# Three split float32r matmuls per product, or one on plain float32: the gate, value and output products of an attention and gated-MLP kernel

## The chip, the cores and the metric

The kernel runs on one core of a Trainium2 chip. The metric is the time of one execution in device microseconds (us); three runs of the kernel before gave 731.21 to 731.88 us with a median of 731.56. The core has five engines that run side by side and meet at semaphores: TensorE (PE in the profile, its weight loads PEld), VectorE (DVE), ScalarE (ACT), GpSimd (POOL) and SyncE (SP), the last of which issues most transfers here.

## The reference

Two stages follow one another. The first is chunked attention with 4 batches, 8 heads, 768 positions and 64 dimensions a head: each chunk of 32 queries sees 8 memory tokens and a window of 56 keys. The second is a gated MLP on the 3072 resulting tokens of 512 features, with an RMS norm ahead of it and a hidden width of 1536. Results are float32.

```
x = attn_out.transpose(0, 2, 1, 3).reshape(B * S, H * D)
rms = np.sqrt(np.mean(x * x, axis=-1, keepdims=True) + 1e-06)
xn = x / rms * rms_g
g = xn @ w_gate
silu = g * (1.0 / (1.0 + np.exp(-g)))
val = xn @ w_val
return (silu * val @ w_out).astype(np.float32)
```

The products called gate, value and output below are `xn @ w_gate`, `xn @ w_val` and the last one. The three weight matrices lie in memory as float64, two 32-bit words to a value, which the kernel turns into float32 itself; all else is float32.

## The kernel before, in words

**Tiling.** The 3072 tokens are cut into 8 blocks (NBLK) of 384 tokens (HT), a block being half a batch. The hidden width is cut into 12 slices f of 128 (NF), the 512 features into 4 slices kt of 128 (NKT). For a block and an f, `moe_in` (L556 to L564) makes the gate product pg and the value product pv, each a 128 x 384 tile of PSUM summed over the 4 kt; the weights are stationary, the block's features xs are moving. `moe_out` (L596 to L600) adds f's share of the output product to three tiles po of 128 tokens x 512 features, one for each 128 tokens of the block; there the hidden values are stationary and the rows of w_out are moving.

**The split.** TensorE is given float32r operands (F32R). Each operand is held as a high part (the value rounded to float32r) and a low part (the rest). `PASS = ((0, 0), (0, 1), (1, 0))` (L554) makes three matmuls of every product: high x high, high x low, low x high. The parts are made as follows.

- Block features: `stage_xt` transposes them on TensorE (xT, L440), `stage_xh` scales them by rms_g into xh (ScalarE or VectorE), `stage_xl` makes xl on VectorE (L450).
- Weights, in 24 chunks: `w_load` (token Z) brings words into a staging tile ws; `w_open`, `w_clamp`, `w_sign` and `w_shift` (J, F, f, I) turn two words into one float32 in a second tile wy; `w_high` (H) casts it into the high part wh on ScalarE, `w_low` (L) subtracts on VectorE and leaves the low part wl (L532).
- Hidden values: `silu_a` (tanh on ScalarE, L568), `silu_b` and `moe_m` (VectorE, L572 and L575) make t; `moe_hh` casts it into hh on ScalarE (L227), `moe_hl` subtracts on VectorE into hl (L584). hh and hl have one buffer each.

With two parts for each weight the weights take twice their size, so those of f 5 to 9 and of f 10 and 11 get their room only when the pools early and stage are closed in the middle of the run (`late_weights`, LATE).

**Order.** The first two blocks run under a written order: the string ORDER (L47 to L64) is a list of tokens, each a step of one engine with its number, and every engine takes its steps in that order. It interleaves the attention of the first eight units with the decoding of the weights and with the first products. W8, W5, W4, W9 and W6 are so many small matmuls on zeros (`warm`, L307). After it, loops over blocks and f issue the work (L857 to L900): gate, value, then the output product of the f before, with the attention of the block after next spread over the gaps; TensorE's order is pinned to the program's, and a planner places the rest. At the end of a block `split_x` makes the next block's features; the last f of the last block goes through `finish`, which works in pieces of 128 tokens.

**Attention on plain float32.** Scores (L318) and attention times values (L368) are plain float32 matmuls already, with 64 stationary columns and 64 or 65 moving ones, and the transposes (L237, L240, L348, L440) are float32 too.

Of the kernel before, what the change touches and what calls it, by code (L numbers as in the profile page):

```python
# [9 lines left out]
F32R = mybir.dt.float32r  # L10
# [13 lines left out]
P = 128  # L24
# [35 lines left out]
l9 I h10 i10 o9 Ha I Z j10 Ha L g11 k10a l10 J L o10 h11 F i11 Z J f v11 L f I F g12 Ha j11 I k11a  # L60
Z J l11 v12 f Ha F L h12 i12 o11 L j12 Z J I g13 f k12a F Ha I v13 L Ha l12 L h13 Z J o12 i13 f
j13 F g14 k13a I l13 Ha L Z J o13 f h14 F I v14 i14 Ha L g15 j14 Z J k14a f l14 F v15 h15 I i15 Ha
g16 j15 J L f F o14 I Ha L v16 k15a l15 h16 o15 i16 j16
# [4 lines left out]
def tile_kernel(ctx: ExitStack, tc: tile.TileContext, q, k, v, mem_k, mem_v,  # L68
# [11 lines left out]
    dram = ctx.enter_context(tc.tile_pool(name="dram", bufs=1, space=bass.MemoryType.DRAM))  # L80
# [5 lines left out]

    def new_weights(pool, a, z):
        for k, (f, n) in enumerate(WGROUPS):
            if a <= f < z:
                for w in "gvo":  # L90
                    for part in range(2):
                        wt[part, w, k] = pool.tile([P, n * DM], F32R, name=f"w{'hl'[part]}_{w}{k}")
    new_weights(const, 0, LATE[0][0])
# [337 lines left out]
    def stage_x(tiles, xh, xl, kt):  # L431

        t = stage_xt(tiles, kt)
        stage_xh(t, xh, kt)
        stage_xl(t, xh, xl, kt)
# [7 lines left out]
    def stage_xh(t, xh, kt, e="a"):  # L443
        if e == "a":
            nc.scalar.activation(xh[:, kt], t[:, 0:HT], AF.Copy, scale=rg[:, kt:kt + 1])
        else:
            nc.vector.tensor_scalar(out=xh[:, kt], in0=t[:, 0:HT], scalar1=rg[:, kt:kt + 1], scalar2=None, op0=ALU.mult)

    def stage_xl(t, xh, xl, kt):
        nc.vector.scalar_tensor_tensor(out=xl[:, kt], in0=t[:, 0:HT], scalar=rg[:, kt:kt + 1], in1=xh[:, kt].bitcast(F32),  # L450
                                       op0=ALU.mult, op1=ALU.subtract)

# [6 lines left out]
    wfirst = [next(c for c, (w, k) in enumerate(wchunks) if WGROUPS[k][0] == late[0]) for late in LATE]  # L459
# [4 lines left out]
    def weight(part, w, f, kt=0):  # L464

        k, i, n = fgroup[f]
        t = wt[part, w, k]
        return t[:, i * DM:(i + 1) * DM] if w == "o" else t[:, (kt * n + i) * P:(kt * n + i + 1) * P]

    def w_load():  # L470
# [6 lines left out]
        d = wst[c] = {}  # L477
        j = c - wfirst[1]
        if j < 0:
            pool = stage if c % 3 else p1  # L480
            tag = str(c % 3) if c % 3 else ""
            s = pool.tile([P, 2, DM, 2], U32, name=f"ws{c}", tag="ws" + tag)
            s = s.rearrange("p n f t -> p (n f) t")[:, 0:n * DM]
        elif j % 3 == 2:
            s = p1.tile([P, DM, 2], U32, name=f"ws{c}", tag="wy")
        else:
            if j % 3 == 0:
                wst["pair"] = p1.tile([P, 2, DM, 2], U32, name=f"ws{c}", tag="ws")
            s = wst["pair"][:, j % 3]
        d.update(n=n, low=s[:, :, 0], high=s[:, :, 1])  # L490
        if w == "o":
            nc.sync.dma_start(out=s.rearrange("p (i f) t -> p i (f t)", i=n),
                              in_=w_out[f * P:(f + n) * P].bitcast(U32).rearrange("(i p) f -> p i f", p=P))
        else:
            src = w_gate if w == "g" else w_val
            nc.sync.dma_start(out=s.rearrange("p (a f) t -> p a (f t)", a=NKT),
                              in_=src.bitcast(U32)[:, 2 * f * P:2 * (f + n) * P].rearrange("(a p) f -> p a f", p=P))

    def w_open(c):

        d = wst[c]
        if c >= wfirst[1]:
            y = obuf(f"wy{c}")
        else:
            pool = stage if c % 3 else p1
            tag = str(c % 3) if c % 3 else ""
            y = pool.tile([P, 2 * DM], F32, name=f"wy{c}", tag="wy" + tag)[:, 0:d["n"] * DM]
# [13 lines left out]
    def w_shift(c):  # L521
        d = wst[c]
# [4 lines left out]
    def w_high(c, e="a"):  # L527
        copy(e, wt[(0,) + wchunks[c]], wst[c]["y"])

    def w_low(c):  # L530
        w = wchunks[c]
        nc.vector.tensor_tensor(out=wt[(1,) + w], in0=wst.pop(c)["y"], in1=wt[(0,) + w].bitcast(F32), op=ALU.subtract)  # L532
        if c + 1 == wfirst[1]:
            stage_cm.__exit__(None, None, None)
            late_weights(1, "left")

    def w_next(fn, *e):

        c = wpos[fn]
        wpos[fn] += 1  # L540
        fn(c, *e)

    wpos.update({fn: 0 for fn in (w_open, w_clamp, w_sign, w_shift, w_high, w_low)})

    def late_weights(i, side):
        late = ctx.enter_context(tc.tile_pool(name=f"late{i}", bufs=1, side=side, reuse_waits="tile"))
        new_weights(late, *LATE[i])

# [5 lines left out]
    PASS = ((0, 0), (0, 1), (1, 0))  # L554

    def moe_in(n, f, xs, last=False):  # L556
        ps = psum_a(f"p{n}") if last else psum_m(n, f"p{n}")
        cnt = 0
        for kt in range(NKT):
            for a, c in PASS:  # L560
                on_pe(nc.tensor.matmul(ps[:, 0:HT], lhsT=weight(a, n, f, kt), rhs=xs[c][:, kt],  # L561
                                 start=cnt == 0, stop=cnt == 3 * NKT - 1))
                cnt += 1
# [10 lines left out]
    def moe_m(t, vv):  # L574
        nc.vector.tensor_tensor(out=t, in0=t, in1=vv, op=ALU.mult)  # L575

    def moe_hh(t, e="a"):
        hh = p1.tile([P, HT], F32R, name="hh", tag="hh")
        copy(e, hh, t)
        return hh  # L580

    def moe_hl(t, hh):
        hl = p1.tile([P, HT], F32R, name="hl", tag="hl")
        nc.vector.tensor_tensor(out=hl, in0=t, in1=hh.bitcast(F32), op=ALU.subtract)  # L584
# [11 lines left out]
    def moe_out(f, h, po):  # L596
        for i in range(NT):
            for n, (a, c) in enumerate(PASS):
                on_pe(nc.tensor.matmul(po[i], lhsT=h[a][:, i * P:(i + 1) * P], rhs=weight(c, "o", f),  # L599
                                 start=f == 0 and n == 0, stop=f == NF - 1 and n == 2))  # L600
# [11 lines left out]
    def finish(f, g, vv, po, blk):  # L612
# [3 lines left out]
        hh = p1.tile([P, HT], F32R, name="hh", tag="hh")  # L616
        hl = p1.tile([P, HT], F32R, name="hl", tag="hl")
        for i in range(NT):
            c = slice(i * P, (i + 1) * P)
            nc.vector.tensor_tensor(out=t[:, c], in0=t[:, c], in1=vv[:, c], op=ALU.mult)  # L620
            nc.scalar.copy(hh[:, c], t[:, c])
            nc.vector.tensor_tensor(out=hl[:, c], in0=t[:, c], in1=hh[:, c].bitcast(F32), op=ALU.subtract)
        for i in range(NT):
            c = slice(i * P, (i + 1) * P)
            o = obuf(f"ob{i}")
            for n, (a, b) in enumerate(PASS):
                on_pe(nc.tensor.matmul(po[i], lhsT=(hh, hl)[a][:, c], rhs=weight(b, "o", f), start=False, stop=n == 2))
# [94 lines left out]
    xs01 = []  # L722
    for i in range(2):
        xs01.append([p1.tile([P, KW + VW], F32R, name=f"x{'hl'[k]}{i}", tag=t)[:, 0:NKT * HT].rearrange("p (a t) -> p a t", a=NKT)
                     if t == "B" else p1.tile([P, NKT, HT], F32R, name=f"x{'hl'[k]}{i}", tag=t)
                     for k, t in enumerate((("xh", "xl"), ("A", "B"))[i])])
# [202 lines left out]
```

## Time and profile before

| | |
|---|---|
| runs shown (three) | 731.21 to 731.88 us, median 731.56 |
| span of the profiled execution | 729.8 us, first to last instruction |
| that execution's own time | not listed apart from the runs |
| TensorE busy | 715.1 us (98%), 5136 matmul records |
| weight loads | 656.6 us (90%) |
| VectorE, ScalarE, GpSimd busy | 380.0, 287.8 and 36.4 us |
| granted TensorE clock, mean | 0.995 of full |
| chain by line | value 28%, output 28%, gate 27% of the span |

The page gives busy time per engine, the span in 40 slices, the chain of work that ended last (followed back from the last instruction), and groups of instructions: line, engine, operation, output and inputs, count, then busy time, mean ns of one, and idle time before it with its releaser. A shape "128*64 128x96" is rows and columns of the stationary operand, then the moving one. In a timeline a row is start, length, engine, line, operation, names, count; in rows by stretch of time it is the stretch, its length, busy time of PE, PEld, DVE, ACT and POOL with counts in brackets, the granted clock, the share of the DMA engines and GB/s. Rows of waits are: who waited, for what, us in total, times, longest.

### The profile page before, as it was taken

The numbers are of one execution on the slowest core, as the hardware profiler recorded it, in microseconds if no ns is written. First come the engines' busy times: TensorE is split into PE (matmuls) and PEld (weight loads), VectorE is DVE, ScalarE is ACT, GpSimd is POOL, SyncE is SP. The second block draws the span as 40 slices with busy tenths as digits, with TensorE's granted clock in tenths as the row PEclk, the third lists the DMA queues.
The fourth block names the chain that finished last, engine by engine and source line by source line (L and its number), as shares of the span: only waits on it lengthen the run. The fifth ranks groups of instructions, "written<-read, shape, count | busy, mean of one in ns | idle before, by whom it ended". The sixth has DMA issues, their size and how long they took to land.

```text
span 729.8 us, 13052 instructions
## 1 busy us (share of the span) xinstructions
PE 715.1 (98%) x5136; PEld 656.6 (90%) x5136; DVE 380.0 (52%) x725; ACT 287.8 (39%) x600; POOL 36.4 (5%) x143
## 2 busy tenths in 40 slices
PE   8889999999999999999999999999999999999997
PEld 7778999999989999899999999989998999999996
DVE  4888999865645443444535353445434543332222
ACT  4899676643452323422333232432234222341112
POOL 3300000001000000000000000000000000000000
PEclk8999999999999999999999999999999999999999
DMA  8994563414412320122212123021311210010001
GB/s 173 203 259 141 173 202 116 132 37 102 85 37 68 55 50 22 62 46 42 43 38 66 23 45 61 20 66 31 66 29 34 64 32 20 20 44 0 1 1 43
DMA packets 143173, 50.20 MB, mean 69 GB/s; under 512 B 126984, under 2 KB 134536, under 8 KB 143112
## 3 DMA queue, kind: packets, MB, share of 16 engines
q1 hardware_dynamic: 139832, 44.49, 26.6%
q10 hardware_dynamic: 3280, 4.88, 1.8%
q8 instruction: 40, 0.66, 0.4%
q14 instruction: 21, 0.17, 0.1%
HBM read 43.06 MB, written 6.29 MB: 68 GB/s over the span
## 4 chain that ended last, share of the span: by engine, by line
PE 92%; ACT 3%; DMA 3%; DVE 1%; issue 0%; POOL 0%; ACTq 0%; SPq 0%; POOLq 0%
PE pv L561 28%; PE po L599 28%; PE pg L561 27%; PE s L318 3%; PE o L368 3%; PE xT L440 1%; PE pT L348 1%; DMA ws<-in_moe_w_val_dram 1%; DMA memV<-in_mem_v_dram 1%; DMA vw<-in_v_dram 1%; ACT junk L398 0%; ACT ws L508 0%; ACT pt L227 0%; DMA kv<-in_v_dram 0%; ACT qb L227 0%
## 5 line engine op out<-in xcount | busy, mean ns | idle before, releaser
L561 PE MATMUL pv<-xh,wh_v 128*128 128x384 f32 x384 | 132.8, 346 | 0.0
L561 PE MATMUL pg<-xh,wh_g 128*128 128x384 f32 x384 | 129.7, 338 | 0.7 <-DVE t L572 0.7
L561 PE MATMUL pv<-xh,wl_v 128*128 128x384 f32 x384 | 129.5, 337 | 0.6 <-DVE wl_v L532 0.6
L561 PE MATMUL pg<-xh,wl_g 128*128 128x384 f32 x384 | 129.5, 337 | 0.0
L561 PE MATMUL pg<-xl,wh_g 128*128 128x384 f32 x384 | 129.3, 337 | 0.0
L561 PE MATMUL pv<-xl,wh_v 128*128 128x384 f32 x384 | 129.3, 337 | 0.0
L572 DVE SCALAR_TENSOR_TENSOR t<-t,pg 128x384 f32<-128x384 f32 x96 | 53.1, 553 | 138.6 <-ACT t L568 138.5
L227 ACT CAST hh<-t 128x384 fp32r<-128x384 f32 x95 | 48.7, 512 | 174.9 <-PE po L599 165.3
L599 PE MATMUL po<-wh_o,hh 128*128 128x512 f32 x285 | 113.8, 399 | 0.3
L599 PE MATMUL po<-wh_o,hl 128*128 128x512 f32 x285 | 113.1, 397 | 0.0
L599 PE MATMUL po<-wl_o,hh 128*128 128x512 f32 x285 | 112.1, 393 | 0.0
L584 DVE TENSOR_TENSOR hl<-t,hh 128x384 fp32r<-128x384 f32 x95 | 52.9, 557 | 100.7 <-ACT hh L227 95.7
L568 ACT ACTIVATE t<-pg 128x384 f32<-128x384 f32 x96 | 47.2, 492 | 135.9 <-PE pg L561 130.8
L575 DVE TENSOR_TENSOR t<-t,pv 128x384 f32<-128x384 f32 x95 | 52.5, 552 | 64.9 <-PE pv L561 64.4
L561 PEld LDWEIGHTS pg<-xh,wh_g 128*128 128x128 f32 x384 | 72.1, 188 | 4.4 <-DVE t L572 0.9
L561 PEld LDWEIGHTS pg<-xl,wh_g 128*128 128x128 f32 x384 | 72.1, 188 | 3.6
L561 PEld LDWEIGHTS pv<-xh,wh_v 128*128 128x128 f32 x384 | 72.1, 188 | 2.4
L561 PEld LDWEIGHTS pv<-xh,wl_v 128*128 128x128 f32 x384 | 72.2, 188 | 0.9 <-DVE wl_v L532 0.9
L561 PEld LDWEIGHTS pv<-xl,wh_v 128*128 128x128 f32 x384 | 72.2, 188 | 0.3
L561 PEld LDWEIGHTS pg<-xh,wl_g 128*128 128x128 f32 x384 | 72.1, 188 | 0.0
L599 PEld LDWEIGHTS po<-wh_o,hl 128*128 128x128 f32 x285 | 53.5, 188 | 14.1 <-DVE hl L584 1.8
L599 PEld LDWEIGHTS po<-wh_o,hh 128*128 128x128 f32 x285 | 53.5, 188 | 10.0 <-ACT hh L227 1.7
(112 smaller groups left out, 772.9 us busy)
## 6 DMA issues: line engine op xcount, KB each, us to landing
kn<-in_k_dram SPq DMA_DIRECT2D x96, 52.0 KB
qn<-in_q_dram SPq DMA_DIRECT2D x96, 48.0 KB
out_dram<-ob ACTq DMA_DIRECT2D x18, 256.0 KB
ws<-in_moe_w_gate_dram SPq DMA_DIRECT2D x4, 1024.0 KB
ws<-in_moe_w_val_dram SPq DMA_DIRECT2D x4, 1024.0 KB
ws<-in_moe_w_out_dram SPq DMA_DIRECT2D x4, 1024.0 KB
kv<-in_v_dram SPq DMA_DIRECT2D x48, 84.0 KB
kv<-in_v_dram SPq DMA_DIRECT2D x48, 70.0 KB
```

Source lines behind the costliest of these rows:

```text
L227: return nc.scalar.copy(out, in_)
L318: on_pe(nc.tensor.matmul(s[64 * par:64 * par + 64, o:o + KC], lhsT=qb[:, c].rearrange("p s q -> p (s q)"), rhs=kw[:, c], start=True, stop= ...
L348: on_pe(nc.tensor.transpose(out=t[:, i * P:(i + 1) * P], in_=pe[:, i * P:(i + 1) * P], identity=ident))
L368: on_pe(nc.tensor.matmul(o[64 * par:64 * par + 64, c0:c0 + D + 1], lhsT=pt[:, i, 2 * par + hh].rearrange("p c q -> p (c q)"), rhs=d["v"][: ...
L440: on_pe(nc.tensor.transpose(out=t[:, i * P:(i + 1) * P], in_=tiles[i][:, kt * P:(kt + 1) * P], identity=ident))
L561: on_pe(nc.tensor.matmul(ps[:, 0:HT], lhsT=weight(a, n, f, kt), rhs=xs[c][:, kt], start=cnt == 0, stop=cnt == 3 * NKT - 1))
L568: nc.scalar.activation(t, g, AF.Tanh, scale=0.5)
L572: nc.vector.scalar_tensor_tensor(out=t, in0=t, scalar=1.0, in1=g, op0=ALU.add, op1=ALU.mult)
L575: nc.vector.tensor_tensor(out=t, in0=t, in1=vv, op=ALU.mult)
L584: nc.vector.tensor_tensor(out=hl, in0=t, in1=hh.bitcast(F32), op=ALU.subtract)
L599: on_pe(nc.tensor.matmul(po[i], lhsT=h[a][:, i * P:(i + 1) * P], rhs=weight(c, "o", f), start=f == 0 and n == 0, stop=f == NF - 1 and n == 2))
```

## The change

Every product is one matmul on float32 operands, where it was three on float32r. The high and low parts are gone: features are one tile xs (two buffers, by turns), hidden values one tile h (two buffers), weights one tile each. The decoded weights are written straight into their final tile, whose room is there from the start; the late pools and their bookkeeping are gone. In ORDER the tokens H, L, D, k and l are struck out; the others keep their sequence.

```
-    PASS = ((0, 0), (0, 1), (1, 0))
+    def product(out, lhsT, rhs, start, stop):
+        on_pe(nc.tensor.matmul(out, lhsT=lhsT, rhs=rhs, start=start, stop=stop))
...
         for kt in range(NKT):
-            for a, c in PASS:
-                on_pe(nc.tensor.matmul(ps[:, 0:HT], lhsT=weight(a, n, f, kt), rhs=xs[c][:, kt],
-                                 start=cnt == 0, stop=cnt == 3 * NKT - 1))
-                cnt += 1
+            product(ps[:, 0:HT], weight(n, f, kt), xs[:, kt], kt == 0, kt == NKT - 1)
...
         for i in range(NT):
-            for n, (a, c) in enumerate(PASS):
-                on_pe(nc.tensor.matmul(po[i], lhsT=h[a][:, i * P:(i + 1) * P], rhs=weight(c, "o", f),
-                                 start=f == 0 and n == 0, stop=f == NF - 1 and n == 2))
+            product(po[i], h[:, i * P:(i + 1) * P], weight("o", f), f == 0, f == NF - 1)
...
     def moe_m(t, vv):
-        nc.vector.tensor_tensor(out=t, in0=t, in1=vv, op=ALU.mult)
-
-    def moe_hh(t, e="a"):
-        hh = p1.tile([P, HT], F32R, name="hh", tag="hh")
-        copy(e, hh, t)
-        return hh
-
-    def moe_hl(t, hh):
-        hl = p1.tile([P, HT], F32R, name="hl", tag="hl")
-        nc.vector.tensor_tensor(out=hl, in0=t, in1=hh.bitcast(F32), op=ALU.subtract)
-        return hh, hl
+        h = p2.tile([P, HT], F32, name="h", tag="h")
+        nc.vector.tensor_tensor(out=h, in0=t, in1=vv, op=ALU.mult)
+        return h
...
-    def stage_xl(t, xh, xl, kt):
-        nc.vector.scalar_tensor_tensor(out=xl[:, kt], in0=t[:, 0:HT], scalar=rg[:, kt:kt + 1], in1=xh[:, kt].bitcast(F32),
-                                       op0=ALU.mult, op1=ALU.subtract)
...
-            y = pool.tile([P, 2 * DM], F32, name=f"wy{c}", tag="wy" + tag)[:, 0:d["n"] * DM]
+        y = wt[wchunks[c]]
...
-    def w_high(c, e="a"):
-        copy(e, wt[(0,) + wchunks[c]], wst[c]["y"])
-
-    def w_low(c):
-        w = wchunks[c]
-        nc.vector.tensor_tensor(out=wt[(1,) + w], in0=wst.pop(c)["y"], in1=wt[(0,) + w].bitcast(F32), op=ALU.subtract)
-        if c + 1 == wfirst[1]:
-            stage_cm.__exit__(None, None, None)
-            late_weights(1, "left")
...
     def finish(f, g, vv, po, blk):
...
-        hh = p1.tile([P, HT], F32R, name="hh", tag="hh")
-        hl = p1.tile([P, HT], F32R, name="hl", tag="hl")
+        h = p2.tile([P, HT], F32, name="h", tag="h")
         for i in range(NT):
             c = slice(i * P, (i + 1) * P)
-            nc.vector.tensor_tensor(out=t[:, c], in0=t[:, c], in1=vv[:, c], op=ALU.mult)
-            nc.scalar.copy(hh[:, c], t[:, c])
-            nc.vector.tensor_tensor(out=hl[:, c], in0=t[:, c], in1=hh[:, c].bitcast(F32), op=ALU.subtract)
+            nc.vector.tensor_tensor(out=h[:, c], in0=t[:, c], in1=vv[:, c], op=ALU.mult)
```

More of the change, by code (lines that the diff above doesn't have):

```diff
@@ new lines @@
+Q2a S1 E0 n2d K2d c2a Z J P0 M1 p5 w2 t3 C0a f m0a S2 a1 Q3a T3 p6 M2 E1 U4 a2 P1 w3 O0 n3d m1a F C1a K3d V4g
+c3a O1 E2 X0 I U5 S3 x0 V5g J X1 u0 U6 P2 x1 M3 p7 W8 C2a Z f m2a w5 a3 O2 u1 E3 V6g P3 X2 t4 F m3a U7 x2 C3a
+I T4 Q4a w6 u2 O3 K4d c4a N0 n4d V7g X3 S4 x3 w4 u3 t5 M4 a4 T5 Q5a T6 c5a n5d Y0 K5d Z K6d t6 w7 n6d c6a y0
+E4 S5 Q6a P4 M5 r0 S6 z0 C4a m4a W4 a5 J M6 t7 E5 f T7 a6 Q7a F P5 n7d K7d m5a A0 c7a I C5a S7 B0a A1 M7 W5
+B1a E6 a7 Z A2 J A3 O4 B2a f W9 X4 E7 B3a x4 P6 F W6 C6a m6a u4 O5 Z J I O6 X5 f P7 g0 X6 x5 x6 u5 C7a m7a u6
@@ new lines @@
+v0 h0 F N1 Z I O7 J X7 i0 x7 g1 j0 u7 Y1 v1 y1 f Z h1 r1 z1 o0 J i1 F j1 A12 A11 I B12a A13 B11a g2 Z B13a A10
+v2 B10a h2 J i2 o1 f j2 g3 J F f v3 I h3 i3 Z o2 f j3 F g4 I v4 h4 i4 J Z F g5 f j4 I o3 v5 F Z J h5 o4 i5 I
+g6 j5 f v6 J Z h6 f o5 i6 F j6 g7 F I J o6 f Z h7 v7 F i7 I g8 j7 I v8 Z h8 i8 J o7 j8 g9 F Z J o8 f h9 f v9 F
+i9 I g10 J j9 Z f F v10 I h10 i10 o9 I Z j10 g11 J o10 h11 F i11 Z J f v11 f I F g12 j11 I Z J v12 f F h12 i12
+o11 j12 Z J I g13 f F I v13 h13 Z J o12 i13 f j13 F g14 I Z J o13 f h14 F I v14 i14 g15 j14 Z J f F v15 h15 I
@@ L64 @@
+i15 g16 j15 J f F o14 I v16 h16 o15 i16 j16
 """
@@ L85, in tile_kernel @@
     wt = {}
[L87 to L93, printed above, removed]
+    for i, (_, n) in enumerate(WGROUPS):
+        for w in "gvo":
+            wt[w, i] = const.tile([P, n * DM], F32, name=f"w_{w}{i}")
     ident = const.tile([P, P], F32, name="ident")
@@ L429, in stage_n, with stage_x @@
         stage_nz(x, sr, "a")
[L431 to L435, printed above, removed]
+    def stage_x(tiles, xs, kt):
+        stage_xh(stage_xt(tiles, kt), xs, kt)
     def stage_xt(tiles, kt):
@@ L441, in stage_xt, with stage_xh @@
         return t
-    def stage_xh(t, xh, kt, e="a"):
+    def stage_xh(t, xs, kt, e="a"):
         if e == "a":
-            nc.scalar.activation(xh[:, kt], t[:, 0:HT], AF.Copy, scale=rg[:, kt:kt + 1])
+            nc.scalar.activation(xs[:, kt], t[:, 0:HT], AF.Copy, scale=rg[:, kt:kt + 1])
         else:
-            nc.vector.tensor_scalar(out=xh[:, kt], in0=t[:, 0:HT], scalar1=rg[:, kt:kt + 1], scalar2=None, op0=ALU.mult)
-    def stage_xl(t, xh, xl, kt):
-        nc.vector.scalar_tensor_tensor(out=xl[:, kt], in0=t[:, 0:HT], scalar=rg[:, kt:kt + 1], in1=xh[:, kt].bitcast(F32),
-                                       op0=ALU.mult, op1=ALU.subtract)
+            nc.vector.tensor_scalar(out=xs[:, kt], in0=t[:, 0:HT], scalar1=rg[:, kt:kt + 1], scalar2=None, op0=ALU.mult)
     LOW = 0.936 * 2.0 ** -29
     wchunks = [(w, k) for k in range(len(WGROUPS)) for w in "gvo"]
-    wfirst = [next(c for c, (w, k) in enumerate(wchunks) if WGROUPS[k][0] == late[0]) for late in LATE]
     fgroup = {f + i: (k, i, n) for k, (f, n) in enumerate(WGROUPS) for i in range(n)}
@@ L462, in tile_kernel, with weight, staged @@
     wpos = {"load": 0}
-    def weight(part, w, f, kt=0):
+    def weight(w, f, kt=0):
         k, i, n = fgroup[f]
-        t = wt[part, w, k]
+        t = wt[w, k]
         return t[:, i * DM:(i + 1) * DM] if w == "o" else t[:, (kt * n + i) * P:(kt * n + i + 1) * P]
+    def staged(c, what, shape, dtype):
+        pool = stage if c % 3 else p1
+        return pool.tile(shape, dtype, name=f"{what}{c}", tag=f"{what}{c % 3}")
     def w_load():
@@ L476, in w_load @@
         f, n = WGROUPS[k]
[L477 to L490, printed above, removed]
+        s = staged(c, "ws", [P, 2, DM, 2], U32).rearrange("p n f t -> p (n f) t")[:, 0:n * DM]
+        wst[c] = dict(n=n, low=s[:, :, 0], high=s[:, :, 1])
         if w == "o":
@@ L525, in w_shift, with w_next @@
                                        op0=ALU.logical_shift_left, op1=ALU.bitwise_or)
-    def w_high(c, e="a"):
-        copy(e, wt[(0,) + wchunks[c]], wst[c]["y"])
-    def w_low(c):
-        w = wchunks[c]
-        nc.vector.tensor_tensor(out=wt[(1,) + w], in0=wst.pop(c)["y"], in1=wt[(0,) + w].bitcast(F32), op=ALU.subtract)
-        if c + 1 == wfirst[1]:
-            stage_cm.__exit__(None, None, None)
-            late_weights(1, "left")
-    def w_next(fn, *e):
+    def w_next(fn):
         c = wpos[fn]
         wpos[fn] += 1
[L541 to L547, printed above, removed]
+        fn(c)
+    wpos.update({fn: 0 for fn in (w_open, w_clamp, w_sign, w_shift)})
     segments = [(0, FC)] + [(blk, 0) for blk in range(2, NBLK)]
-    PASS = ((0, 0), (0, 1), (1, 0))
+    def product(out, lhsT, rhs, start, stop):
+        on_pe(nc.tensor.matmul(out, lhsT=lhsT, rhs=rhs, start=start, stop=stop))
     def moe_in(n, f, xs, last=False):
         ps = psum_a(f"p{n}") if last else psum_m(n, f"p{n}")
-        cnt = 0
         for kt in range(NKT):
-            for a, c in PASS:
-                on_pe(nc.tensor.matmul(ps[:, 0:HT], lhsT=weight(a, n, f, kt), rhs=xs[c][:, kt],
-                                 start=cnt == 0, stop=cnt == 3 * NKT - 1))
-                cnt += 1
+            product(ps[:, 0:HT], weight(n, f, kt), xs[:, kt], kt == 0, kt == NKT - 1)
         return ps[:, 0:HT]
@@ L625, in finish @@
             o = obuf(f"ob{i}")
-            for n, (a, b) in enumerate(PASS):
-                on_pe(nc.tensor.matmul(po[i], lhsT=(hh, hl)[a][:, c], rhs=weight(b, "o", f), start=False, stop=n == 2))
+            product(po[i], h[:, c], weight("o", f), False, True)
             rows = slice(blk * HT + i * P, blk * HT + (i + 1) * P)
@@ L721, in tile_kernel @@
     blk = {"x": x}
[L722 to L726, printed above, removed]
+    xs01 = [p1.tile([P, NKT, HT], F32, name=f"xs{i}", tag=f"xs{i}") for i in range(2)]
     def xtiles(x):
@@ L807, in tile_kernel @@
         O=stage_o, X=stage_ra, x=stage_rb, u=tok_u,
-        N=tok_N, e=tok_e, Y=tok_Y, y=tok_y, z=tok_z, r=tok_r, A=tok_A, B=tok_B, D=tok_D,
-        g=tok_g, v=tok_v, h=tok_h, i=tok_i, j=tok_j, k=tok_k, l=tok_l, o=tok_o,
+        N=tok_N, e=tok_e, Y=tok_Y, y=tok_y, z=tok_z, r=tok_r, A=tok_A, B=tok_B,
+        g=tok_g, v=tok_v, h=tok_h, i=tok_i, j=tok_j, o=tok_o,
         J=lambda n: w_next(w_open), F=lambda n: w_next(w_clamp), f=lambda n: w_next(w_sign),
-        I=lambda n: w_next(w_shift),
-        H=lambda n, *e: w_next(w_high, *e), L=lambda n, *e: w_next(w_low, *e))
-    early_open = True
+        I=lambda n: w_next(w_shift))
     for tok in ORDER.split():
-        if early_open and wpos[w_high] == wfirst[0] and tok[0] == "H":
-            early_cm.__exit__(None, None, None)
-            late_weights(0, "right")
-            early_open = False
         e = tok[-1] if tok[1:] and tok[-1].isalpha() else ""
         steps[tok[0]](int(tok[1:len(tok) - len(e)] or 0), *e)
+    early_cm.__exit__(None, None, None)
+    stage_cm.__exit__(None, None, None)
     ends = [next(i for i in reversed(nc.cur_bb.bb.instructions) if i.engine == eng)
@@ L837, in tile_kernel, with split_x @@
     pinned.append(True)
-    def split_x(x, first, rest):
-        xh = p1.tile([P, NKT, HT], F32R, name="xh", tag="xh")
-        xl = p1.tile([P, NKT, HT], F32R, name="xl", tag="xl")
+    def split_x(x, n, first, rest):
+        xs = p1.tile([P, NKT, HT], F32, name=f"xs{n}", tag=f"xs{n % 2}")
         with tc.high_priority():
@@ L846, in split_x @@
                     first()
-                stage_x(xtiles(x), xh, xl, kt)
+                stage_x(xtiles(x), xs, kt)
         rest()
-        return xh, xl
+        return xs
     last1 = len(SEQ) - 1
```

46 lines of the change are left out of this document (8 added, 38 removed).

## The prediction

> **What bounds the kernel now.** I read the page first: the busy share of each engine, the clock row, the chain of work that ended last, and the costliest groups.
>
> ```profile
> span 729.8 us, 13052 instructions
> PE 715.1 (98%) x5136; PEld 656.6 (90%) x5136; DVE 380.0 (52%) x725; ACT 287.8 (39%) x600; POOL 36.4 (5%) x143
> PEclk8999999999999999999999999999999999999999
> ...
> PE 92%; ACT 3%; DMA 3%; DVE 1%; issue 0%; POOL 0%; ACTq 0%; SPq 0%; POOLq 0%
> PE pv L561 28%; PE po L599 28%; PE pg L561 27%; PE s L318 3%; PE o L368 3%; PE xT L440 1%; PE pT L348 1%; DMA ws<-in_moe_w_val_dram 1%; DMA memV<-in_mem_v_dram 1%; DMA vw<-in_v_dram 1%; ACT junk L398 0%; ACT ws L508 0%; ACT pt L227 0%; DMA kv<-in_v_dram 0%; ACT qb L227 0%
> ...
> L561 PE MATMUL pv<-xl,wh_v 128*128 128x384 f32 x384 | 129.3, 337 | 0.0
> L227 ACT CAST hh<-t 128x384 fp32r<-128x384 f32 x95 | 48.7, 512 | 174.9 <-PE po L599 165.3
> L599 PE MATMUL po<-wh_o,hh 128*128 128x512 f32 x285 | 113.8, 399 | 0.3
> L584 DVE TENSOR_TENSOR hl<-t,hh 128x384 fp32r<-128x384 f32 x95 | 52.9, 557 | 100.7 <-ACT hh L227 95.7
> ```
>
> TensorE is busy 98% of the span at full clock, and 83% of the chain are the three products. VectorE and ScalarE are half idle, and their idle time ends with TensorE: what they do is hidden, and what TensorE's own stream costs decides. Matmul records overlap (337 ns is the life of one record, not its share of the time), so I take the share from the chain in order of time, where a piece ends where the next one starts.
>
> ```profile
> 74.92 2.08 PE pv L561 x12
> 77.00 2.09 PE po L599 x9
> 79.10 2.09 PE pg L561 x12
> ```
>
> Twelve split matmuls of 384 columns take 2.085 us (174 ns each, 0.4525 ns per column), nine of 512 columns 2.09 us (232 ns, 0.4536 per column). Per block and per f there is one such gate, value and output group; 8 blocks x 12 f = 96, so the products take 96 x (2.085 + 2.085 + 2.09) = **601.0 us** of the 729.8.
>
> **What the change takes out and puts in on TensorE.** 3 x 1056 split matmuls become 1056 on plain float32 (768 of 384 columns, 288 of 512). The kernel has no plain float32 product of that size, but it has small ones. First, how many records one makes, from the groups kept apart by shape:
>
> ```profile
> L318 PE MATMUL s<-kv,qp 128*64 128x64 f32 x576 | 23.2, 228 | 0.0
> L440 PE MATMUL xT<-ident,x 128*128 128x128 f32 x96 | 13.5, 274 | 0.2 <-ACT qb L227 0.2
> L307 PE MATMUL warm<-zero 128*64 128x64 f32 x64 | 4.7, 224 | 0.0
> ```
>
> The 24 later units have 12 score products each at L318: 288 matmuls, 576 records. The warm-up tokens W8, W5, W4, W9 and W6 ask for 32 matmuls at L307 and leave 64. So a plain float32 product runs as **two** records; a transpose (L440: 8 blocks x 4 x 3 = 96) runs as one. Second, what one record costs, from the timeline of TensorE. The warm-ups are the cleanest row, because the score products run two side by side in the two halves of the array:
>
> ```profile
> 46.20 1.21 PE L307 MATMUL warm<-zero 128*64 128x64 f32 x18
> ```
>
> The last of 18 records lives 0.222, so 17 gaps take 1.21 - 0.22 = 0.99 us: **58.1 ns for 64 columns**, 0.908 ns per column. That is 2.0 times the split form's 0.4525, and there are two of them: a plain product costs about four passes against three. It remains to be settled how 58.1 grows to 384 and 512 columns. Float32 transposes have two more widths, and one stretch ran at half clock (timeline, then two stretches of time with their granted clock):
>
> ```profile
> 18.10 0.85 PE L237 MATMUL qT<-ident,qf 96*128 96x96 f32 x4
> 18.74 0.85 PE L240 MATMUL qT<-ident,qf 96*64 96x96 f32 x4
> ...
> 32.51 0.52 PE L237 MATMUL kT<-ident,kf 104*128 104x104 f32 x4
> 33.58 0.52 PE L240 MATMUL kT<-ident,kf 104*64 104x104 f32 x4
> ...
> 644.13 1.14 PE L440 MATMUL xT<-ident,x 128*128 128x128 f32 x9
> ```
>
> ```profile
> 18.10:19.40 1.30, 1.30 (x9) 1.14 (x8) 1.03 (x2) 1.11 (x3) 0.00 (x0) 0.50 1.02 336
> 32.10:33.90 1.80, 1.80 (x23) 1.77 (x21) 1.51 (x3) 1.76 (x6) 0.00 (x0) 1.00 1.19 145
> ```
>
> At clock 0.50 four transposes of 96 columns take 18.74 - 18.10 = 0.64 us: 160 ns each, 1.667 ns per column, so 0.8333 at full clock. At full clock 104 columns take (33.58 - 32.51) / 12 = 89.2 ns (three groups of four between those starts), that is 86.7 + 2.5; 128 columns take (1.14 - 0.27) / 8 = 108.5, that is 106.7 + 1.8. A transpose is thus 0.8333 ns per column and a fixed 2. Read in the same way, the float32 product is 64 x 0.8333 = 53.3 and a fixed 4.8. I take this form, because both are float32 and its fixed part holds over two widths. Then:
>
> - 384 columns: 320.0 + 4.8 = 324.8 per record, 649.6 per matmul, against 3 x 174 = 521 now;
> - 512 columns: 426.7 + 4.8 = 431.5 per record, 863.0 per matmul, against 697 now;
> - per block and f: 8 x 0.6496 + 3 x 0.8630 = 7.786 us against 6.26; times 96 = 747.5. **Plus 146.5 us.**
>
> Bounds: with the transposes' fixed 2 it is 742 (plus 141). With 58.1 growing in proportion, as the split form does (0.4525 at 384 and 0.4536 at 512, no fixed part to be seen), it is 348.6 and 464.8 per record, 8.367 us per block and f, 803.2 in all: plus 202.2. Below nothing: the two rivals further down.
>
> **What goes elsewhere.** Removed beside hl (52.9 us of VectorE) and hh (48.7 of ScalarE):
>
> ```profile
> L450 DVE SCALAR_TENSOR_TENSOR xl<-xT,rg,xh 128x384 fp32r<-128x384 f32 x32 | 18.6, 612 | 3.0 <-ACT xh L445 2.6
> L532 DVE TENSOR_TENSOR wl_v<-wy,wh_v 128x512 fp32r<-128x512 f32 (+1 forms) x8 | 7.6, 952 | 1.0 <-ACT wh_v L227 1.0
> L227 ACT CAST wh_v<-wy 128x512 fp32r<-128x512 f32 (+1 forms) x8 | 6.6, 830 | 2.2 <-DVE wy L524 2.1
> ```
>
> The last two stand once each for w_gate, w_val and w_out, so VectorE loses 52.9 + 18.6 + 3 x 7.6 = 94 us and ScalarE 48.7 + 3 x 6.6 = 69. All of it is covered by TensorE, except in the front, where these engines feed it, and in the tail. Waits of TensorE up to 66 us, the two stretches where VectorE and ScalarE are fullest, and the tail's timeline:
>
> ```profile
> PE pT L348 <- DVE r L386: 1.3, 1, 1.3
> PE qT L237 <- ACT junk L398: 0.8, 1, 0.8
> PE pg L561 <- DVE t L572: 0.7, 1, 0.7
> PE pv L561 <- DVE wl_v L532: 0.6, 1, 0.6
> ```
>
> ```profile
> 24.00:30.00 6.00, 5.77 (x105) 4.96 (x99) 6.00 (x16) 4.51 (x10) 2.76 (x7) 1.00 1.11 204
> 30.00:36.00 6.00, 4.27 (x66) 3.89 (x67) 4.70 (x13) 5.09 (x19) 1.25 (x3) 1.00 1.06 190
> 36.00:42.00 6.00, 4.96 (x79) 4.06 (x74) 4.64 (x11) 5.85 (x12) 0.61 (x1) 1.00 0.85 148
> ...
> 200.00:400.00 200.00, 198.95 (x1405) 182.35 (x1404) 90.83 (x184) 69.20 (x160) 8.74 (x34) 1.00 0.22 48
> ```
>
> ```profile
> 723.26 0.70 ACT L621 CAST hh<-t 128x128 fp32r<-128x128 f32 x3 [3.46 <-PE po L599]
> 723.61 0.50 PE L627 MATMUL po<-wh_o,hh 128*128 128x512 f32 x1 [0.15 <-ACT hh L621]
> ```
>
> The wait for wl_v goes (0.6); in the tail the cast that waits until the last L599 record has let go of the single buffer hh goes (723.26 to 723.61: 0.35), since h has two buffers. In the front VectorE (6.00 of 6) and ScalarE (5.85 of 6) are full about where TensorE idles: 3.0 us in the three stretches from 24 to 42, and after them 2.6 in the waits for r, t and wl_v. With casts and subtractions gone I credit half of these 5.6 as 3 us. Together **minus 4**, with bounds of 0 (the front's loads set it) and minus 8 (nearly all its idle time goes). After 66 us TensorE idles about 1 us in 200; there the removed work is worth nothing, and longer products only cover more. What the new tokens move on SyncE is nothing: the loads Z keep their order, and a stage buffer is still let go by w_shift (L521 to L525). The h and xs tiles have two buffers each, so no wait is added; if one were, the cover is a value and an output group, 2 x 2.6 us, over tanh and two VectorE steps of about 0.5 each.
>
> Sum: the span 729.8 + 146.5 - 4 = 872.3. The runs shown (731.21 to 731.88, median 731.56) lie about 1.8 above the span; with that it is **874 us**. The median stands for the profiled execution's own time here.
>
> The Trainium skill says, in "FP8 and Floating Point Precision", section "TensorE Precision Notes", that true FP32 takes four passes through the array (high and low part of each operand). The two records of double price agree. Four passes at the split form's own 174 and 232 ns would be the proportional 202 us.
>
> **Rivals.**
>
> *Proportional growth* (B). The record costs 0.908 ns per column at any width: 731.6 + 202.2 - 4 = **930**. For it: 0.908 is almost exactly twice 0.4525, as if both suffered from one cause. Against it: the split form's records are the only ones that take a column per beat; a float32 record has two beats for a column, as a transpose has, and those show a fixed part alone.
>
> *Single rate* (C), the other side. In 58.1 ns I count 64 columns at two beats. It could be 64 columns of weights and 64 moving ones at one beat each (half of 0.8333, 0.4167 ns), with the load in the open. Then a record of the new products takes (384 + 128) x 0.4167 + 4.8 = 218 or (512 + 128) x 0.4167 + 4.8 = 271.5; per block and f 5.12 us, in all 491: minus 110, and **618 us**. It decides from the point where a record of 384 columns is under 260 ns. Against it: L237 and L240 above load 128 and 64 weight columns and take the same 0.64 us at half clock, so loads don't show; those are transposes, which leaves it a little chance.
>
> *Half rate* (D). Each of the two records runs at the split form's price: 2 x 174 and 2 x 232, 4.17 us per block and f, 400.6 in all, minus 200: **527 us**. Against it: the 58.1 ns, for which a record of 64 columns would have to be 29. The Trainium skill, in "Perfetto Trace Analysis", section "Engine Utilization", halves the array's output rate for FP32_LOW_HIGH; read as the price of the whole product, that is this case. The row of 18 records contradicts it, unless the rate is meant per record.
>
> *Open weight loads* (E). 128 weight columns of 0.4167 ns before each of 2112 records, nothing hidden: 53.3 ns x 2112 = 113 us on top of the forecast, **987**. Against it the rows of the loads:
>
> ```profile
> L440 PEld LDWEIGHTS xT<-ident,x 128*128 128x128 f32 x96 | 11.3, 141 | 2.0 <-ACT qb L227 0.4 <-issue 0.3
> L561 PEld LDWEIGHTS pv<-xl,wh_v 128*128 128x128 f32 x384 | 72.2, 188 | 0.3
> ```
>
> A float32 load of 128 columns lives 141 ns, less than the split form's 188, and would lie under a record of 325. The Trainium skill, in "TensorE: Matmul & The Clock Gate", section "Weight-path perf modes", gives fast weight load to all types but FP32. That speaks against this change, but the loads' rows show no longer life for float32.
>
> **How the numbers follow.** Forecast (A) 0.70, B 0.19, E 0.04, C 0.03, D 0.03, anything within 0.2% 0.01 (0.2% is about what a measurement of this kernel tells from no change). Slower is A, B and E: 0.93; faster C and D: 0.06. A's own range is 864 (plus 141, minus 8, rounded down) to 878 (no credit for the front). A alone holds 7 in 10, so the range has to reach to B: to 937, B without the front's credit and a little. 864 to 937.
>
> **What would show it.** 2112 records of the gate, value and output products, two per matmul, with 4 gate matmuls taking 2.60 us in the chain and 3 output matmuls 2.59 (B: 2.79 and 2.79; C: 1.75 and 1.63). TensorE stays at 98% or more with the chain on the same lines; VectorE falls to some 286 us busy, ScalarE to some 219; the first gate product begins a few us before the one of now:
>
> ```profile
> 51.80 0.42 PE L561 MATMUL pg<-xh,wh_g 128*128 128x384 f32 x1
> ```
>
> It is wrong if a record of 384 columns is not between 322 and 349 ns after its neighbour, or if TensorE gets idle stretches after 70 us.

## The result, and the profile after

The changed kernel takes 866.53 us, the median of four runs (865.95 to 870.3), against 731.72 before in the same comparison. It is 1.185 times as long, with a 95% interval of 1.182 to 1.187. The forecast was 874 us in a range of 864 to 937.

The page of the changed kernel, the lines that answer to those shown of before:

```profile
span 868.6 us, 10600 instructions
PE 852.4 (98%) x4080; PEld 493.4 (57%) x4080; DVE 291.5 (34%) x571; ACT 221.7 (26%) x478; POOL 36.5 (4%) x143
...
PE pv L501 29%; PE pg L501 29%; PE po L501 29%; PE s L306 3%; PE o L356 3%; PE pT L336 1%; PE xT L425 1%; DMA ws<-in_moe_w_out_dram 1%; DMA ws<-in_moe_w_gate_dram 1%; DMA kf<-in_k_dram 1%; DMA memV<-in_mem_v_dram 1%; DMA vw<-in_v_dram 1%; PE kT L225 0%; SPq L144 0%; PE warm L295 0%; PE kT L228 0%
...
L501 PE MATMUL pv<-xs,w_v 128*128 128x384 f32 x768 | 266.6, 490 | 0.0
L501 PE MATMUL po<-w_o,h 128*128 128x512 f32 x576 | 263.1, 593 | 0.0
```

TensorE is still the bound, busy for 98% of a longer span at a mean granted clock of 0.994, with the same three products on the chain. There are 768 records for 384 value matmuls and 576 for 288 output matmuls: two for each. VectorE lost 88 us of work and ScalarE 66, and the run did not get shorter for it. The pieces of its chain in order of time:

```profile
79.78 2.58 PE pg L501 x8
82.36 2.58 PE pv L501 x8
84.94 2.57 PE po L501 x6
```

Four matmuls of 384 columns take 2.58 us where the split took 2.085, three of 512 take 2.57 where it took 2.09. Per block and f that is 7.735 us (2.575 for the output group, the mean of the 2.57 and 2.58 that its pieces show) against 6.26, and 96 times the difference is 141.6 us.

### The profile page after: what moved, and what is told of

It reads as the page before. It is cut to its first block, busy times and chain, and to the rows that moved or that the text cites. A ratio compares the mean times of both kernels' runs of the same rounds, so it can differ in the third digit from the quotient of the medians.

```text
span 868.6 us, 10600 instructions
## 1 busy us (share of the span) xinstructions
PE 852.4 (98%) x4080; PEld 493.4 (57%) x4080; DVE 291.5 (34%) x571; ACT 221.7 (26%) x478; POOL 36.5 (4%) x143
## 4 chain that ended last, share of the span: by engine, by line
PE 95%; DMA 3%; ACT 0%; POOL 0%; DVE 0%; SPq 0%; issue 0%; ACTq 0%; POOLq 0%
PE pv L501 29%; PE pg L501 29%; PE po L501 29%; PE s L306 3%; PE o L356 3%; PE pT L336 1%; PE xT L425 1%; DMA ws<-in_moe_w_out_dram 1%; DMA ws<-in_moe_w_gate_dram 1%; DMA kf<-in_k_dram 1%; DMA memV<-in_mem_v_dram 1%; DMA vw<-in_v_dram 1%; PE kT L225 0%; SPq L144 0%; PE warm L295 0%; PE kT L228 0%
## 5 line engine op out<-in xcount | busy, mean ns | idle before, releaser
L501 PE MATMUL pv<-xs,w_v 128*128 128x384 f32 x768 | 266.6, 490 | 0.0
L501 PE MATMUL pg<-xs,w_g 128*128 128x384 f32 x768 | 263.6, 486 | 0.7 <-DVE t L515 0.7
L501 PE MATMUL po<-w_o,h 128*128 128x512 f32 x576 | 263.1, 593 | 0.0
L501 PEld LDWEIGHTS pg<-xs,w_g 128*128 128x128 f32 x768 | 145.7, 190 | 118.7 <-issue 35.9
L501 PEld LDWEIGHTS pv<-xs,w_v 128*128 128x128 f32 x768 | 143.3, 190 | 96.9 <-issue 3.4
L501 PEld LDWEIGHTS po<-w_o,h 128*128 128x128 f32 x576 | 108.2, 190 | 113.5 <-issue 92.1
L519 DVE TENSOR_TENSOR h<-t,pv 128x384 f32<-128x384 f32 x95 | 52.5, 552 | 107.0 <-PE pv L501 107.0
L275 DVE STREAM_TRANSPOSE qp<-qn 64x384 f32<-64x384 f32 x48 | 27.2, 567 | 0.8
L481 DVE SCALAR_TENSOR_TENSOR ws<-ws 128x512 uint32<-128x512 uint32 (+1 forms) x24 | 22.7, 955 | 5.5 <-ACT ws L471 5.5
L306 PE MATMUL s<-kv,qp 128*64 128x64 f32 x576 | 23.2, 228 | 0.0
```

Source lines behind the costliest of these rows:

```text
L275: nc.vector.transpose(out=qb[64 * hh:64 * hh + 64, :, hh, :], in_=d["q"][64 * hh:64 * hh + 64])
L306: on_pe(nc.tensor.matmul(s[64 * par:64 * par + 64, o:o + KC], lhsT=qb[:, c].rearrange("p s q -> p (s q)"), rhs=kw[:, c], start=True, stop= ...
L481: nc.vector.scalar_tensor_tensor(out=d["low"], in0=d["high"], scalar=0x80000000, in1=d["low"], op0=ALU.bitwise_and, op1=ALU.bitwise_or)
L501: on_pe(nc.tensor.matmul(out, lhsT=lhsT, rhs=rhs, start=start, stop=stop))
L519: nc.vector.tensor_tensor(out=h, in0=t, in1=vv, op=ALU.mult)
```

## The experiments

**Price of one matmul by itself.** A row of 24 equal matmuls for each width and type, on one set of operands, and none of the reference's work (f is float32, r float32r, h float16; a name ends in m with 128 stationary columns, in h with 64 of them, and float16 has only m):

```
+    for n in (64, 128, 256, 384, 512):
+        series(f"f{n}m", w, x[:, 0:n])
+        series(f"f{n}h", w[:, 0:64], x[:, 0:n])
+    series("fz", w, z[:, 0:384])
+    for n in (256, 384, 512):
+        series(f"r{n}m", wr, xr[:, 0:n])
+        series(f"r{n}h", wr[:, 0:64], xr[:, 0:n])
...
+    for n in (128, 256, 384, 512):
+        series(f"h{n}m", wh, xh[:, 0:n])
```

> TensorE alone, nothing of the reference is computed (the output is zeros): 24 equal matmuls in a row for each of several widths, on plain float32, float32r and float16, with 128 and with 64 stationary columns, and two rows on zeros. Forecast (fixed part): a float32 record starts 0.8333 ns x columns + a fixed 2 to 5 ns after the one before, so 322 to 325 ns at 384 columns and 429 to 432 at 512, whatever the stationary columns. Proportional growth: 0.908 ns per column, 349 and 465 ns. Open weight loads: 128 stationary columns take some 50 ns more than 64 at every width. Float32r: if its 174 and 232 ns are a fixed part, 256 columns take about 121 ns (107 + 14); if they are proportional, 116.

Timeline of TensorE (start, length, engine, line, operation, names, stationary and moving shape, records):

```profile
27.00 5.57 PE L50 MATMUL f64m<-x,w 128*128 128x64 f32 x48
32.63 3.01 PE L50 MATMUL f64h<-x,w 128*64 128x64 f32 x48
35.70 5.62 PE L50 MATMUL f128m<-x,w 128*128 128x128 f32 x48
41.39 5.45 PE L50 MATMUL f128h<-x,w 128*64 128x128 f32 x48
...
68.22 15.75 PE L50 MATMUL f384m<-x,w 128*128 128x384 f32 x48
84.02 15.69 PE L50 MATMUL f384h<-x,w 128*64 128x384 f32 x48
99.77 20.87 PE L50 MATMUL f512m<-x,w 128*128 128x512 f32 x48
120.70 20.81 PE L50 MATMUL f512h<-x,w 128*64 128x512 f32 x48
141.57 15.75 PE L50 MATMUL fz<-z,w 128*128 128x384 f32 x48
157.47 3.11 PE L50 MATMUL r256m<-xr,wr 128*128 128x256 f32 x24
160.63 2.95 PE L50 MATMUL r256h<-xr,wr 128*64 128x256 f32 x24
163.64 4.44 PE L50 MATMUL r384m<-xr,wr 128*128 128x384 f32 x24
168.14 4.38 PE L50 MATMUL r384h<-xr,wr 128*64 128x384 f32 x24
172.58 5.74 PE L50 MATMUL r512m<-xr,wr 128*128 128x512 f32 x24
178.38 5.74 PE L50 MATMUL r512h<-xr,wr 128*64 128x512 f32 x24
...
190.23 2.78 PE L50 MATMUL h256m<-xh,wh 128*128 128x256 f16 x24
193.07 4.06 PE L50 MATMUL h384m<-xh,wh 128*128 128x384 f16 x24
197.19 5.34 PE L50 MATMUL h512m<-xh,wh 128*128 128x512 f16 x24
```

From 384 to 512 columns a float32 record grows by (20.87 - 15.75) / 48 = 106.7 ns, 0.8333 ns per column and no more: the form with a fixed part holds, proportional growth doesn't. Stationary columns hardly matter at 384 (15.75 and 15.69) and 512 (20.87 and 20.81), so loads are hidden there. At 64 moving columns they set the time: 128 stationary columns take 5.57 where 64 take 3.01, 53 ns more per record, which is 0.8333 ns for each of the 64 more; and 64 or 128 moving columns behind 128 stationary ones take the same (5.57, 5.62). Moving operands of zero change nothing (fz). Float16 grows by 0.417 ns per column ((5.34 - 4.06) / 24 / 128); call this a beat, so that a float32 column takes two. Behind 128 stationary columns float32r grows by 0.42 to 0.43 ((5.74 - 4.44) and (4.44 - 3.11) in the same way) and takes 14 to 17 ns more than float16 at each width (3.11 - 2.78, 4.44 - 4.06 and 5.74 - 5.34 over 24). There its distance from a beat per column looks like a fixed part, and not like the 8% that 174 and 232 ns suggested. Behind 64 stationary columns it grows by 0.47 and 0.44 (from 2.95, 4.38 and 5.74), so what makes up this distance stays open.

**Four split passes.**

```
-    PASS = ((0, 0), (0, 1), (1, 0))
+    PASS = ((0, 0), (0, 1), (1, 0), (1, 1))
...
```

> The kernel before with a fourth split product, low x low, added to the three: four float32r matmuls per product, nothing else changed. If time goes by passes at the split form's price, the products grow from 601.0 to 801 us and the run takes 932 us; this is what four passes would cost if the plain form had no price of its own. Against the 866.5 us of the changed kernel it tells how much of a plain product is the number of its passes and how much their price. Rival: the two are the same, 866.

Measured 928.96 us (1.269 of before, 1.265 to 1.273). Two pieces of its chain:

```profile
304.13 2.98 PE pv L561 x16
307.11 2.80 PE po L599 x12
```

The second piece is 12 x 0.233; the first follows the attention's matmuls and starts slower (16 x 0.174 would be 2.78). Four passes in the split form cost 197 us over before, against 135 for the changed kernel: the plain products save 62 of them, or 58 against the kernel below that keeps the split's other work too (871.17, in the same comparison). This is about what a record takes beyond its beats: 2.5 ns for each of a plain matmul's two records (322.5 against 320), for each of four split matmuls 14 ns at 384 columns (174 against 160) and 19 at 512 (232 against 213). With 4 x 14 = 56, 4 x 19 = 76 and 2 x 2.5 = 5, 96 x (8 x (56 - 5) + 3 x (76 - 5)) ns, for 8 matmuls of 384 and 3 of 512 columns in each of 96 groups, are 59.6 us.

**Two split passes.**

```
-    PASS = ((0, 0), (0, 1), (1, 0))
+    PASS = ((0, 0), (0, 1))
...
```

> The kernel before with two split products, high x high and high x low; low x high is left out of the computation. If TensorE's stream alone sets the time, 601.0 us of products become 400.7 and the run takes 531 us. Rival: with a third of the cover gone, the chain tanh, two VectorE steps, cast and subtraction ends last in each f; with half a microsecond of wait in each of 96 groups it is 580 us.

Measured 571.01 us (0.779, 0.776 to 0.782): 40 more than TensorE's stream alone. Busy time by stretch (PE, PEld, DVE, ACT, then GpSimd where it worked, clock, DMA share, GB/s), and the longest wait of TensorE:

```profile
66.00:100.00 34.00, 28.06 (x131) 22.92 (x131) 33.10 (x46) 24.73 (x34) 0.00 (x0) 0.95 0.48 155
100.00:200.00 100.00, 85.41 (x551) 74.37 (x552) 80.20 (x141) 55.82 (x108) 4.86 (x22) 0.93 0.46 119
200.00:400.00 200.00, 197.32 (x1534) 179.28 (x1533) 126.03 (x255) 91.43 (x209) 11.11 (x47) 1.00 0.30 63
```

```profile
PE pg L561 <- DVE t L572: 11.6, 11, 2.1
```

It lies between the two forecasts, and neither had the place. TensorE idles 20 us between 66 and 200, while VectorE, which still decodes the weights there, is busy for 33.1 of the first 34 us; after 200 the chain that the rival named costs little (2.7 us of idle in 200). In the kernel before VectorE is as full from 66 to 100 (32.66 us), but TensorE has enough to do there (34.00). So with a third of the products gone, VectorE's decoding probably sets the pace in that stretch: its lines L514, L518 and L524 hold 21% of the chain between 66 and 200, and have no part in it before. No run took the decoding away. Of the other 20 us, the granted clock of 0.95 and 0.93 there and a front in which TensorE is busy 4.7 us less up to 66 (51.78 for 56.49) are a part. The change goes the other way and gives VectorE more cover.

**Products plain, the split's work kept.** Each product is one float32 matmul on the high parts; every cast and subtraction stays.

```
-            for a, c in PASS:
-                on_pe(nc.tensor.matmul(ps[:, 0:HT], lhsT=weight(a, n, f, kt), rhs=xs[c][:, kt], ...
+            on_pe(nc.tensor.matmul(ps[:, 0:HT], lhsT=weight(0, n, f, kt).bitcast(F32), rhs=xs[0][:, kt].bitcast(F32),
+                                   start=kt == 0, stop=kt == NKT - 1))
...
```

> The kernel before with one plain float32 matmul per product, taken on the high parts read as float32; every cast and subtraction of the split is still done, on the same engines and in the same order, and the low parts are not used, so the low-order terms are missing from the result. If the price is TensorE's and the removed work of the other engines is worth only the front and the tail, the time is 731.7 + 96 x (2 x 2.58 + 2.573 - 6.26) = 873 us, 6 to 7 above the changed kernel. Rival: the removed work is worth nothing, and it takes 866.5 like the changed kernel.

Measured 871.17 us (1.189, 1.186 to 1.192). That lies 4.6 above the changed kernel's 866.53, but the two stand in different comparisons; so it was run again beside the changed kernel.

> The kernel before with one plain float32 matmul per product on the high parts and all casts and subtractions kept (low-order terms missing), again, beside the changed kernel on one chip. If the removed work of VectorE and ScalarE is worth the 6 us that the sum leaves for front and tail, it is 4 to 7 us above the changed kernel, 871 to 873; if it is worth nothing, the two are equal.

> The changed kernel once more, as the base for the next two. 866.5 us. Its first profile shows the first gate product at 55.82 us, later than the 51.80 of before, behind a wait of 3.5 us for ScalarE, and its run was the longest of four (870.3); if that is the rare case, a second profile has the first gate product at 51 to 53 us and a span near 864.

Measured 870.38 us (1.188, 1.186 to 1.191) and 865.58 us (1.182, 1.180 to 1.184): the removed work is worth **4.8 us** of some 154 taken from two engines. The place is the end of a block. First the chain of the kernel with the split's work kept, then the changed kernel's:

```profile
765.98 2.59 PE po L596 x6
768.57 0.02 issue
768.60 0.52 ACT hh L227
769.12 0.04 issue
769.16 2.84 PE po L596 x6
```

```profile
763.32 2.58 PE po L501 x6
765.90 0.33 PE xT L425 x3
766.23 2.58 PE po L501 x6
```

At a block's end two output products follow each other with no gate and value between. The cast into hh has one buffer and starts only when the first of the two has let go of it, and the second waits for the cast: from 768.57 to 769.16, 0.59 us in place of the 0.33 of transposes that it hides, and its first records start slower (2.84 for 2.58). That is 0.52 us an end. There are six such ends, 3.1 us, and the tail's wait adds 0.4:

```profile
PE po L623 <- ACT hh L618: 0.4, 1, 0.4
```

These are 3.5 of the 3.8 us between the two spans (869.2 and 865.4); the medians are 4.8 apart, and the last us of these has no place in the profiles.

**One buffer or two.** The same place, tried from both sides.

```
-        hh = p1.tile([P, HT], F32R, name="hh", tag="hh")
+        hh = p2.tile([P, HT], F32R, name="hh", tag="hh")
...
```

> The kernel with one plain matmul on the high parts and the split's casts kept (low-order terms missing), with two buffers for hh instead of one. Theory: its 4.8 us over the changed kernel are six block ends, where ScalarE's cast of hh waits until the output product of the f before has let go of the one buffer, and TensorE waits for the cast (0.82 us each, 4.9 in all). Then it takes 865.5 us, like the changed kernel. Rival: the casts and subtractions themselves cost the time, 870.

Measured 867.1 us (1.184, 1.182 to 1.185), where it was 1.188 with one buffer. The chain at a block's end is now the changed kernel's:

```profile
454.44 0.33 PE xT L440 x3
454.77 2.58 PE po L596 x6
```

All casts and subtractions are still done; with hh late no more, they cost nothing that this comparison tells. The length of a block says the same: from the first transpose of one block end to that of the next it is 103.32 us here (347.40 to 450.72), 103.32 in the changed kernel (348.89 to 452.21) and 103.86 with the split's work kept and one buffer (349.42 to 453.28). The other way round, the changed kernel with one buffer for h:

```
-        h = p2.tile([P, HT], F32, name="h", tag="h")
+        h = p1.tile([P, HT], F32, name="h", tag="h")
...
```

> The changed kernel with one buffer for h instead of two, nothing else. Theory: the wait at the six block ends and in the tail comes back, now for VectorE's multiply (0.55 us and two semaphores, some 0.85 us each with the restart of the products): 5 to 6 us more, 871. Rival: the second buffer is not what removed the wait, 865.6.

Measured 871.28 us (1.189, 1.188 to 1.191), 5.3 by the ratio over the changed kernel. Its chain at a block's end has the multiply where the cast was:

```profile
457.27 0.57 DVE h L519
```

And the kernel before with a second hh:

> The kernel before with two buffers for hh (hl keeps one; two of each don't fit in SBUF). At its block ends TensorE stands 0.45 us in all (the wait and the longer restart), six times: 2.7 us less if hh is what it waits for, 729.5; if hl is the next to be late, since its subtraction still waits for the buffer, 732.

Measured 731.17 us beside 732.86 (0.998, 0.997 to 0.999): 1.7 us less. An end of a block in the kernel before, and with the second buffer:

```profile
647.37 0.33 PE xT L440 x3
647.69 0.04 issue
647.73 2.50 PE po L599 x9
```

```profile
390.30 0.33 PE xT L440 x3
390.62 2.20 PE po L599 x9
```

The second output product shrinks from 2.50 to 2.20 and the issue gap goes: 0.34 us, six times 2.0, with 0.11 still open (2.09 is its length elsewhere). The timeline of that second product has the 0.11 where hl is first read:

```profile
390.95 0.50 PE L599 MATMUL po<-wh_o,hl 128*128 128x512 f32 x1
...
391.74 0.40 PE L599 MATMUL po<-wh_o,hl 128*128 128x512 f32 x1
```

The record after the first on hl starts 0.33 us behind it (391.28), the one after the second on hl 0.23 (391.97). So hl is late next. A second buffer for it was not tried in float32r, for lack of room in SBUF; the float16 split below has it.

**The front's order.** The first profile of the changed kernel, taken in the only long one of its four runs (870.3 us), has this in its front (waits; a stretch with the clock third from last; timeline):

```profile
PE pT L336 <- ACT xs L430: 3.5, 1, 3.5
```

```profile
48.00:54.00 6.00, 3.73 (x46) 3.40 (x48) 3.66 (x6) 5.85 (x9) 0.00 (x0) 0.58 0.92 325
```

```profile
55.82 2.75 PE L501 MATMUL pg<-xs,w_g 128*128 128x384 f32 x8
```

ScalarE stands at a weight chunk that is still loading (3.19 us, until its step on ws at 47.61), the features queue behind it, TensorE waits for these, and its granted clock is 0.58 in the mean of these 6 us (0.50 from 50 to 55 us). One step of the order was moved:

```
-B1a E6 a7 Z A2 J A3 O4 B2a f W9 X4 E7 B3a x4 P6 F W6 C6a ...
+B1a E6 a7 Z A2 A3 O4 B2a W9 X4 E7 B3a J x4 P6 f F W6 C6a ...
```

> The changed kernel with one step of the written order moved: the step that opens the fourth weight chunk (J, with its f) comes after the block's last features (B3a) on ScalarE instead of ahead of B2a. Theory: ScalarE stands at the chunk's load while TensorE waits for the features, so the front gets up to 3.3 us shorter, 863 us, most of it in executions where that load is late. Rival: the loads set the front anyway and the second gate product waits instead, 866.5.

Measured 865.82 us (1.183, 1.181 to 1.185) beside the changed kernel's 865.58: no difference, though in its profile the first gate product starts at 51.01 us. In the changed kernel's second profile the wait is 0.2 us and the first gate product starts here:

```profile
52.62 2.75 PE L501 MATMUL pg<-xs,w_g 128*128 128x384 f32 x8
```

So the 3.5 us belong to single executions, and the order is not what makes the kernel slower.

**Float16 for the split.** The rows of widths point to a form of the split that takes less beyond its beats.

```
-F32R = mybir.dt.float32r
+F16 = mybir.dt.float16
...
-                        wt[part, w, k] = pool.tile([P, n * DM], F32R, name=f"w{'hl'[part]}_{w}{k}")
+                        wt[part, w, k] = pool.tile([P, n * DM], F16, name=f"w{'hl'[part]}_{w}{k}")
...
```

> The kernel before with float16 in place of float32r for the high and low parts, three matmuls per product as before; low parts of weights below float16's normal range lose accuracy. By the row of widths a float16 matmul of 384 columns starts 162.2 ns after the one before and one of 512 columns 215.7, so a block and f takes 24 x 0.1622 + 9 x 0.2157 = 5.83 us instead of 6.26: 96 x 0.43 = 41 us less, 691 us. Rival: the half microsecond waits that the two-product run showed come up, 710.

Measured 691.3 us (0.944, 0.943 to 0.946), as forecast. Two pieces of its chain:

```profile
307.37 1.94 PE po L599 x9
309.31 1.95 PE pg L561 x12
```

With two buffers for hh and hl, which now fit:

> The float16 split with two buffers for hh and hl, three matmuls per product; low parts of weights below float16's normal range lose accuracy. The profile of the float16 split stands 0.33 us after each of six block ends' transposes instead of 0.11, and the restart costs 0.1 more: 2 to 3 us less than 691.3, 688.8. If the cast and the subtraction are needed in the open at the block's end whatever the buffers, 691.3.

Measured 688.42 us (0.939, 0.938 to 0.940), as forecast. The second output product at a block's end is now as long as the others:

```profile
610.92 1.94 PE po L599 x9
```

This is the shortest of the kernels that keep all three products, and it beats both. How much accuracy the small low parts of the weights lose was not measured.

## Why the prediction was right, and where it was not

- *TensorE's stream sets the time, and the removed work is covered.* Right. Kept whole, with hh given a second buffer, that work is not to be told from none (1.184 and 1.182, intervals that touch).
- *Two records per matmul, each two beats for a column.* Right: 2.58 / 8 = 322.5 ns at 384 columns, two beats for each being 320, and 2.57 / 6 = 428 at 512, where they are 427. The Trainium skill's four passes, in "FP8 and Floating Point Precision", section "TensorE Precision Notes", agree: 645 ns a matmul are four times 161, and one beat for each of 384 columns is 160. The halved rate of "Perfetto Trace Analysis", section "Engine Utilization", holds only if it is read per record; there are two, and rival D is out.
- *The fixed part of 4.8 ns.* This is the term that was mis-sized. It is 322.5 - 320.0 = 2.5, as in the transposes, so by their typical pieces the products cost 141.6 us more and not 146.5. The warm-ups that it was read from have as many stationary as moving columns, and in such a record the load takes part: with 128 moving columns, 128 stationary ones cost (5.62 - 5.45) / 48 = 3.5 ns more than 64. The same shape, 64 by 64, in the row of widths takes 58 ns again. The bound with the transposes' fixed part (plus 141) is what came. Of the 6.9 us by which the forecast span of 872.3 lies above the 865.4 of the second profile, 4.9 are this term; the other 2.0 are the credit for front and tail.
- *Rival B, proportional growth.* Out by the row of widths. What spoke for it, 0.908 being twice 0.4525, was a coincidence of two extras: that of the square shape in the one, some 14 to 19 ns per matmul in the other.
- *Rivals C and E, loads in the open.* Out at 384 and 512 columns, where 64 and 128 stationary columns take the same. At 64 moving columns loads do set the time, but not as C had it: one beat for each of 128 stationary and 64 moving columns would be 80 ns and a fixed part of 4.8, and 112 were measured. The Trainium skill, in "TensorE: Matmul & The Clock Gate", section "Weight-path perf modes", denies float32 the fast load; the 53 ns for 64 more stationary columns fit that, and under a record of 322 ns they are hidden.
- *Minus 4 for front and tail.* The size was near by luck, the place was wrong. The spans differ by 865.4 - 729.8 = 135.6 us, 6.0 less than the products' 141.6. The front shows no gain: the first gate product starts at 52.62 us instead of 51.80, and profiles with the changed kernel's front scatter from 50.99 (with one h) to 55.82. What went is the wait for hh at six block ends, (0.04 + 2.50 - 2.09) x 6 = 2.7 us, and the same wait in the tail, 0.35. The prediction had seen that wait in the tail alone, and had taken the block ends for covered. Of the remaining 3 us, 0.6 are the wait for wl_v and 0.8 a wait of the attention for a load, which the changed kernel's two profiles do not have. The rest is no gain at all: the price before was taken from short pieces. Others last 2.11 us, and over the run the gate and value records inside a stretch of products start 174.6 ns apart where the sum has 173.75, which for 2179 of them is 1.8 us. All this makes 6.2, so the account is closed to a few tenths. The lines, of the kernel before:

```profile
PE o L368 <- DMA kv<-in_v_dram: 0.8, 1, 0.8
```

```profile
706.78 2.11 PE pv L561 x12
```

- *Busy time.* VectorE 291.5 and ScalarE 221.7, for 286 and 219.

## What to carry to other kernels

A plain float32 matmul is two records of two beats per column, so at 384 and 512 columns three float32r or float16 matmuls are shorter than one float32 matmul here, and dropping casts and subtractions that TensorE covers gives nothing back. Read a price for a large matmul from a row whose stationary side is smaller than its moving side, and use several widths; a square one shows the load. When work is removed, look for its gain where two uses of one buffer follow each other closely, such as the end of a block, and try a second buffer before removing the work.

## What the runs showed of the hardware that was not expected

Float32r takes 14 to 17 ns more per matmul than float16 at 256, 384 and 512 columns behind 128 stationary ones (the differences of the rows of 24), so the same three-product split is 41 us shorter in float16 (732.6 to 691.3). Float32 weight loads take 0.8333 ns per column, two beats, and set the time below about as many moving as stationary columns (112 ns from record to record for 64 or 128 moving columns behind 128 stationary ones, the medians in the rows of 5.57 and 5.62 us). Moving operands that are all zero take exactly the time of others behind the same stationary ones (15.75 us for both rows).
